# A decode kernel with attention cache and MLP: fewer loads of the output weights, another order of the last matmuls, and bias loads moved

## The chip, the cores and the metric

The kernel runs on one core of a Trainium2 chip. The metric is the device time of one execution in microseconds (us). The engines of the core run side by side: TensorE (PE) does matmuls, VectorE (DVE), ScalarE (ACT) and GpSimd (POOL) the elementwise work, and SyncE (SP) issues nearly all transfers from device memory. Those transfers run on 16 DMA engines that the core has to itself.

## The reference

One token for each of 8 sequences. `x` (8 x 448) goes through two branches whose results are mixed with a gate:

```
g = sigmoid((x * gate_w).sum(-1))
a = attention(x, k_cache, v_cache, wq, wo)   # 16 query heads, 8 key heads of 256,
                                             # the last 1024 of 4096 cache rows, softmax
b = gelu(layernorm(x) @ w1 + b1) @ w2 + b2   # 448 -> 1792 -> 448
out = g * a + (1 - g) * b                    # 8 x 448, bf16
```

All inputs are bf16. The parts of the two caches that are read are eight loads of 4096 KB each; `wq` and `wo` have 3584 KB each. In all 77.69 MB are read, and each byte of the caches is used for one sequence only.

## The kernel before

**Loads and the ring.** A ring of four large SBUF buffers (`slot`, 4 MB each) takes the loads in the order of a list (`plan`, lines 163 to 180): `wq`; eight blocks of keys (`quarter_loader`, L120), from the fifth on in turn with the values of one sequence each (`pair_loader`, L130); the remaining values; `w1`; the last values together with `w2` (`last_values`, L159); and `wo` in several pieces. `pump` (L103) issues the next load of the list on SP as soon as a buffer has been given back by `done`. SP runs its queue in order, so a load that waits holds up all behind it. A completion of a load is signalled through one of eight semaphores, which the loads take in turn; a load that takes a semaphore waits until the one that had it before has landed, unless SP knows that already.

**`wo`.** It is used as 32 chunks of 128 rows: four blocks (`q`) of 8 chunks (`J8`). `cuts` (L172) says which chunks come in one load: each of the first two blocks is one load of 896 KB, the third comes in two of 448 KB, the fourth in pieces of 2, 4, 1 and 1 chunks.

**Biases.** `biases` (L193) issues on SP `b2`, broadcast to 8 rows of `b2_b` in two loads of 4 rows, and `b1` in four loads of one row. It is called in the main loop at the second key block (L661, `m == 1`). They are first read in `norm` (L318), long after.

**Main loop** (L659). Each key block is turned on PE, or on DVE and POOL, into `kt` (`transpose_keys`), scored against all queries (`scores`), and from the fifth block on (`KQ` = 4) the softmax and the values of an earlier sequence follow (`steps`, `values`). For each sequence, `finish` and `spread` put the attention result into `oP`, in the layout in which it is a stationary operand. `mlp_hidden` (L593) makes `hs`, the 14 hidden chunks of the MLP branch, already scaled by 1 - g.

**The end** (L688 to 740). The output is a sum of 46 products: 14 chunks of `hs` by `w2` and 32 of `oP` by `wo`. `chunks` lists them in that order. All but the last `TAIL` = 12 are "wide": a matmul of 448 columns each, accumulated in four groups of PSUM partitions of `A1` in turn. When they are done, DVE adds the groups' tile and `b2s` into `accs` (L719). The last 12 are "narrow": each is two matmuls of 224 columns, one for each half of the output, into `A2[0]` or `A2[1]` as the list `part` says. Both are pieces of the one PSUM tile `S_ps`. A product `pick` by `accs` (fp32), put in at place `EARLY` of the narrow list, adds the four groups of the wide part. When the last product for `A2[1]` is done, DVE copies it to `early` (L737); at the very end DVE adds `A2[0]` and `early` into `res` (L738), and two stores write the halves (L740).

**Fillers.** `run_on(n)` (L698) issues matmuls with no use into a PSUM tile `warm`; `FILL` says after how many wide chunks how many of them come, and one of 256 columns stands ahead of the copy to `early`.

Of the kernel before, what the change touches and what calls it, by code (L numbers as in the profile page):

```python
# [12 lines left out]
F32 = mybir.dt.float32  # L13
# [4 lines left out]
def kernel(  # L18
# [15 lines left out]
    nc = tc.nc  # L34
    P = nc.NUM_PARTITIONS

    NB, Sq, D = A_x.shape
# [8 lines left out]
    QD = 4  # L46
    BL = P // QD
# [10 lines left out]
    QN = 512  # L58
# [5 lines left out]
    DO = D // 2  # L64
    J8 = Dh // BL
    NQW = Hq // QD
# [6 lines left out]
    CK = SLOT // Dh  # L73
    KQ = W // (KS * CK)
    HR = GROUP * UR
    TAIL = 12
    SHIFT = 96
    EARLY = 4
    TURNED = {5: 3, 6: 3, 7: 3}
    FAR = -3.0e38  # L80
    FILL = {0: 3, 14: 5, 22: 4, 30: 1, 34: 1}
    qscale = float(Dh) ** -0.5

    xf = A_x.rearrange("b s d -> (b s) d")
# [3 lines left out]
    consts = ctx.enter_context(tc.tile_pool(name="consts", bufs=1))  # L88
# [3 lines left out]
    work = ctx.enter_context(tc.tile_pool(name="work", bufs=1))  # L92
    spool = ctx.enter_context(tc.tile_pool(name="spool", bufs=2))
    ps_s = ctx.enter_context(tc.tile_pool(name="ps_s", bufs=1, space=PSUM))
    ps_kt = ctx.enter_context(tc.tile_pool(name="ps_kt", bufs=3, space=PSUM))
# [17 lines left out]
    def add(key, loader):  # L113
        index[key] = len(plan)
        plan.append(loader)

    def slot(*key):
        return slots[index[key]]
# [49 lines left out]
    for b in range(KQ, NB - 1):  # L168
        add(("v", b), pair_loader(A_v_cache, b))
    add(("w12",), rows_loader([w1_m, w1_t]))  # L170
    add(("v", NB - 1), last_values)
    cuts = [(q, 0, J8) for q in range(NQW - 2)] + [  # L172
        (NQW - 2, 0, 4),
        (NQW - 2, 4, 8),
        (NQW - 1, 0, 2),
        (NQW - 1, 2, 6),
        (NQW - 1, 6, 7),
        (NQW - 1, 7, 8),
    ]
# [7 lines left out]
    b2_b = consts.tile([NB, D], BF16)  # L187
# [2 lines left out]
        g_b[:], gate_w.rearrange("(o d) -> o d", o=1).to_broadcast([NB, D])  # L190
    )

    def biases():  # L193
        for o in range(0, NB, QD):
            nc.sync.dma_start(
                b2_b[o : o + QD, :],
                B_b2.rearrange("(o d) -> o d", o=1).to_broadcast([QD, D]),
            )
        parts = B_b1.rearrange("(t d) -> t d", t=QD)
        for t in range(QD):  # L200
            nc.sync.dma_start(b1_r[BL * t : BL * t + 1, :], parts[t : t + 1, :])

    ident = consts.tile([P, P], BF16)
    make_identity(nc, ident[:])
# [3 lines left out]
    S_ps = ps_s.tile([P, NG * W], F32)  # L208
# [19 lines left out]
    for u in range(NG):  # L228
        o = u * BL
# [31 lines left out]
    mask = consts.tile([P, QD, rep], F32)  # L261
    gall = consts.tile([P, NB], F32)
    oall = consts.tile([P, NB], F32)
    pick = consts.tile([P, NB], F32)
    om = consts.tile([NB, 1], F32)
    b1_b = consts.tile([P, FQ], BF16)

# [8 lines left out]
    def gate():  # L276
        prod = consts.tile([NB, D], F32)
        gl = consts.tile([NB, 1], F32)
        nc.vector.scalar_tensor_tensor(
            prod[:],  # L280
            in0=x_sb[:],
            scalar=1.0,
            in1=g_b[:],
            op0=ALU.mult,
            op1=ALU.mult,
            accum_out=gl[:],
        )
        gth = consts.tile([NB, 1], F32)
        nc.scalar.activation(gth[:], gl[:], ACT.Tanh, scale=0.5)
        nc.vector.tensor_copy(  # L290
            perm[:].rearrange("p (s a) -> p s a", a=QD),
            ident[:].rearrange("p (a s) -> p s a", a=QD),
        )
        nc.vector.reduce_sum(
            pick[:],
            ident[:].rearrange("p (g b) -> p b g", g=QD)[:, 0:NB, :],
            axis=AXIS.X,
        )
        nc.vector.reduce_sum(
            mask[:],  # L300
            ident[:]
            .rearrange("p (s o a) -> p a o s", a=QD, o=1)
            .to_broadcast([P, QD, rep, SK]),
            axis=AXIS.X,
        )
        nc.vector.tensor_scalar(
            g32[0:NB, 0:1], gth[:], 0.5, 0.5, op0=ALU.mult, op1=ALU.add
        )
        nc.vector.tensor_scalar(om[:], gth[:], -0.5, 0.5, op0=ALU.mult, op1=ALU.add)
        gt = consts.tile([BL, BL], F32)  # L310
        nc.vector.transpose(gt[:], g32[:])
        gb = consts.tile([BL, BL], F32)
        nc.vector.stream_shuffle(gb[:], gt[:], [0] * BL)
        for i in range(QD):
            nc.scalar.copy(gall[BL * i : BL * (i + 1), :], gb[:, 0:NB])
        nc.vector.tensor_scalar(oall[:], gall[:], -1.0, 1.0, op0=ALU.mult, op1=ALU.add)
# [34 lines left out]
    def turn_blocks(m):  # L351
        kn = slot("k", m)[:].bitcast(F32)
        n = TURNED.get(m, 1) * CB
        B = epool.tile([P, n, QD, BL], F32, tag="B", name="B")
        nc.vector.transpose(  # L355
            B[:].rearrange("p c w x -> p (c w x)"),
            kn[:, 0 : n * P],
        )
        blocks[m] = B
# [14 lines left out]
    def transpose_keys(m, between):  # L374
        kn = slot("k", m)[:].bitcast(F32)
        kt = ktpool.tile([P, P, CK, NJ], BF16, tag="kt", name="kt")
        KT[0] = kt
        n = TURNED.get(m, 1)
        for g in range(CK // CB):
            if g < n:  # L380
                if g == 0:
                    spread_blocks(m, kt)
                for step in between.get(g, ()):
                    step()
                continue
            ktp = ps_kt.tile([P, CB, P, NJ], BF16, tag="ktp", name="ktp")
            words = ktp[:].bitcast(F32)
            for c in range(CB):
                o = (g * CB + c) * P
                nc.tensor.transpose(words[:, c, :, 0], kn[:, o : o + P], ident_f[:])  # L390
            dst = kt[:, :, g * CB : (g + 1) * CB, :]
            src = ktp[:].rearrange("p c x t -> p x c t")
            if g in BY_ACT[m // KQ]:
                nc.scalar.copy(dst, src)  # L394
            else:
                nc.vector.tensor_copy(dst, src)  # L396
            for step in between.get(g, ()):
                step()
        done()
# [76 lines left out]
    def top(g):  # L476
        nmx = spool.tile([P, 1], F32, tag="nmx", name="nmx")
        nc.vector.reduce_max(nmx[:], S_ps[:], axis=AXIS.X, negate=True)  # L478
        soft[-1 - g] = nmx
# [161 lines left out]
    def steps(b):  # L641
        if b == 0:
            return {
                3: [lambda: expo(0, 0)],
                5: [lambda: expo(0, 1)],
                8: [lambda: turn(0)],
                10: [lambda: scale(0)],
                12: [lambda: bring(0)],
            }
        return {  # L650
            5: [lambda: scale(b)],
            7: [lambda: bring(b)],
            9: [lambda: finish(b - 1)],
            12: [lambda: spread(b - 1)],
        }
# [3 lines left out]
    for m in range(NK):  # L659
        transpose_keys(m, steps(m - KQ) if m >= KQ else {})  # L660
        if m == 1:  # L661
            biases()
        if m < KQ:
            turn_blocks(m + 1)
        if m == 0:
            gate()
        scores(m)
        if m % KQ == KQ - 1:
            top(m // KQ)
        if m >= KQ:  # L670
            values(m - KQ)
# [13 lines left out]
    finish(b)  # L685
    spread(b)

    A2 = [S_ps[:, k * QN : k * QN + DO] for k in range(2)]  # L688
    warm = ps_kt.tile([P, QN], F32, tag="ktp", name="warm")
    w2 = slot("w12")  # L690
    w = slot("wo")
# [3 lines left out]
    ] + [(oP[:, c % J8, c // J8, :], w[:, c * D : (c + 1) * D]) for c in range(NCH)]  # L695
    wide, narrow = chunks[:-TAIL], chunks[-TAIL:]

    def run_on(n, m=QN):  # L698
        for _ in range(n):
            nc.tensor.matmul(  # L700
                warm[:, 0:m],
                lhsT=ident[:],
                rhs=slot("v", NB - 1)[:, 0:m],
                start=True,
                stop=True,
            )

    run_on(FILL[0])
    for i, (lhsT, rhs) in enumerate(wide):
        g = i % QD  # L710
        nc.tensor.matmul(
            A1[BL * g : BL * g + NB, :],
            lhsT=lhsT,
# [3 lines left out]
        )  # L717
        run_on(FILL.get(i + 1, 0))
    nc.vector.tensor_tensor(accs[:], A1[:], b2s[:], op=ALU.add)  # L719
    narrow.insert(EARLY, (pick[:], accs[:]))  # L720
    part = [1, 0, 1, 0, 0, 1, 1, 0, 0, 0, 0, 0, 0]
    early = consts.tile([2 * BL, DO], F32)
    res = consts.tile([2 * BL, DO], BF16)
    for i, (lhsT, rhs) in enumerate(narrow):
        k = part[i]
        for h in range(2):
            g = 2 * k + h
            nc.tensor.matmul(
                A2[k][BL * g : BL * g + NB, :],
                lhsT=lhsT,  # L730
                rhs=rhs[:, h * DO : (h + 1) * DO],
                start=(k not in part[:i]),
                stop=(k not in part[i + 1 :]),
            )
        if 1 not in part[i + 1 :] and k == 1:
            run_on(1, QN // 2)
            nc.vector.tensor_copy(early[:], A2[1][2 * BL : P, :])  # L737
    nc.vector.tensor_tensor(res[:], A2[0][0 : 2 * BL, :], early[:], op=ALU.add)  # L738
    for h, eng in enumerate((nc.sync, nc.scalar)):
# [31 lines left out]
```

## Time and profile before

| | us |
|---|---|
| median of 3 runs | 189.43 |
| lowest and highest run | 189.4, 189.66 |
| the profiled execution, its own time | 189.29 |
| span of its instructions | 187.4 |
| PE busy (share of the span) | 125.4 (67%) |
| DVE busy | 94.0 (50%) |
| POOL busy | 80.8 (43%) |
| ACT busy | 72.4 (39%) |
| wo, loads of 896 KB, 448 KB, 224 KB, 112 KB | 2, 3, 1, 2 of them |

The span is the time from the first to the last instruction in the profile; the whole execution is 1.9 us longer. Busy shares are averages over stages with different limits. In the page's slices each digit is the busy share of one fortieth of the span in tenths, with 9 for 90% and more; "DMA" is the mean over the 16 DMA engines. In the chain of waits each step is followed back to what released it. In the timeline a line gives start, duration, engine, source line, operation, output and inputs, and in brackets how long the engine was idle before and what ended that.

### The profile page before, as it was taken

The numbers are of one execution on the slowest core, as the hardware profiler recorded it, in microseconds if no ns is written. First come the engines' busy times: TensorE is split into PE (matmuls) and PEld (weight loads), VectorE is DVE, ScalarE is ACT, GpSimd is POOL, SyncE is SP. The second block draws the span as 40 slices with busy tenths as digits, with TensorE's granted clock in tenths as the row PEclk, the third lists the DMA queues.
The fourth block names the chain that finished last, engine by engine and source line by source line (L and its number), as shares of the span: only waits on it lengthen the run. The fifth ranks groups of instructions, "written<-read, shape, count | busy, mean of one in ns | idle before, by whom it ended". The sixth has DMA issues, their size and how long they took to land.

```text
span 187.4 us, 2775 instructions
## 1 busy us (share of the span) xinstructions
PE 125.4 (67%) x1102; PEld 73.0 (39%) x1103; DVE 94.0 (50%) x161; ACT 72.4 (39%) x87; POOL 80.8 (43%) x157
## 2 busy tenths in 40 slices
PE   0252498998988988489877985984670167543983
PEld 0010485675756746253752572563120022111321
DVE  6602247664654566770662281493044982347611
ACT  2003379692855929740680373184025010001000
POOL 8401591671927639103996899299900000000000
PEclk9999579999999999756997899999576576855798
DMA  6999999999998999999999999999999999999991
GB/s 223 444 455 448 448 434 413 388 442 448 444 448 381 418 439 435 430 416 455 451 416 402 434 458 441 392 441 427 430 430 423 434 430 428 432 430 418 421 406 65
DMA packets 5443, 77.85 MB, mean 415 GB/s; under 512 B 540, under 2 KB 1080, under 8 KB 1848
## 3 DMA queue, kind: packets, MB, share of 16 engines
q1 hardware_dynamic: 5384, 77.68, 97.2%
q8 instruction: 8, 0.13, 0.2%
q10 hardware_dynamic: 48, 0.02, 0.0%
q14 instruction: 3, 0.02, 0.0%
HBM read 77.69 MB, written 0.01 MB: 415 GB/s over the span
## 4 chain that ended last, share of the span: by engine, by line
DMA 46%; PE 25%; ACT 12%; DVE 7%; POOL 5%; issue 2%; SPq 1%; POOLq 0%; ACTq 0%; DVEq 0%
DMA slot<-in_A_k_cache_dram 22%; PE ktp L390 15%; DMA slot<-in_B_w_dram 12%; DMA slot<-in_A_wo_dram 12%; ACT kt L394 9%; PE S_ps L465 7%; POOL kt L369 5%; DVE kt L396 3%; PE PO L550 2%; DVE B L355 1%; ACT E L489 1%; ACT other L489 1%; SPq L143 1%; DVE EB L505 1%; DVE E L503 1%
## 5 line engine op out<-in xcount | busy, mean ns | idle before, releaser
L369 POOL COPY kt<-B 32x128 f32<-32x128 f32 (+1 forms) x128 | 72.4, 566 | 42.8 <-PE S_ps L465 24.9
L390 PE MATMUL ktp<-ident_f,slot 128*128 128x128 f32 x456 | 64.6, 292 | 14.0 <-DMA slot<-in_A_k_cache_dram 5.9
L394 ACT COPY kt<-ktp 128x1024 bf16<-128x1024 bf16 x57 | 56.3, 1015 | 45.8 <-PE ktp L390 45.7
L390 PEld LDWEIGHTS ktp<-ident_f,slot 128*128 128x128 f32 x456 | 52.4, 148 | 27.7 <-ACT kt L394 11.3
L396 DVE COPY kt<-ktp 128x1024 bf16<-128x1024 bf16 x57 | 39.0, 689 | 32.0 <-PE ktp L390 31.6
L465 PE MATMUL S_ps<-kt,qw 128*16 128x512 bf16 x256 | 21.1, 458 | 12.1 <-POOL kt L369 9.3
L550 PE MATMUL PO<-slot,ET 128*16 128x512 bf16 x256 | 22.2, 508 | 6.6 <-DMA slot<-in_A_v_cache_dram 3.0
L355 DVE STREAM_TRANSPOSE B<-slot 128x512 f32<-128x512 f32 (+1 forms) x8 | 8.8, 1105 | 14.2 <-DMA slot<-in_A_k_cache_dram 9.7
L465 PEld LDWEIGHTS <-qw 128*16 128x16 bf16 x256 | 6.6, 92 | 23.8 <-issue 13.3
L550 PEld LDWEIGHTS <-ET 128*16 128x16 bf16 x256 | 7.9, 112 | 19.3 <-issue 12.9
L525 PE MATMUL sm<-EZ,perm 128*128 128x128 bf16 x8 | 2.0, 248 | 13.4 <-DVE EZ L512 13.4
L407 PE MATMUL S_ps<-slot,xw 128*8 128x512 bf16 x24 | 2.9, 618 | 10.7 <-DVE xw L254 7.1
L478 DVE TENSOR_REDUCE nmx<-S_ps 128x1 f32<-128x2048 f32 x2 | 4.6, 2292 | 9.8 <-PE S_ps L465 9.8
L565 DVE STREAM_TRANSPOSE T<-PO 128x512 f32<-128x512 f32 x8 | 5.7, 707 | 7.6 <-PE PO L550 7.6
L627 ACT ACTIVATE zb<-za 128x448 f32<-128x448 f32 x1 | 0.6, 576 | 18.8 <-DVE za L626 18.8
L489 ACT ACTIVATE E<-S_ps,nmx 128x1024 f32<-128x1024 f32 x2 | 4.1, 2031 | 9.7 <-DVE nmx L478 9.7
L525 PEld LDWEIGHTS <-perm 128*128 128x128 bf16 x8 | 0.8, 100 | 16.6 <-DVE EZ L512 16.6
L445 POOL COPY qw<-qt 32x64 bf16<-32x64 bf16 x8 | 2.2, 277 | 11.3 <-DVE qt L432 11.0
L533 DVE TENSOR_TENSOR ET<-sm,mask 128x512 bf16<-128x512 f32 x8 | 5.5, 687 | 1.1 <-PE sm L525 1.0
L432 DVE STREAM_TRANSPOSE qt<-qs 128x512 bf16<-128x512 bf16 x2 | 1.3, 690 | 8.8 <-ACT qs L429 8.8
L407 PEld LDWEIGHTS <-xw 128*8 128x8 bf16 x24 | 0.7, 100 | 12.0 <-POOL b_r L237 7.1
L700 PE MATMUL warm<-slot,ident 128*128 128x512 bf16 (+1 forms) x14 | 4.3, 392 | 0.1
(91 smaller groups left out, 69.0 us busy)
## 6 DMA issues: line engine op xcount, KB each, us to landing
slot<-in_A_k_cache_dram SPq DMA_DIRECT2D x8, 4096.0 KB, 24.6
slot<-in_A_v_cache_dram SPq DMA_DIRECT2D x8, 4096.0 KB, 30.0
slot<-in_A_wq_dram SPq DMA_DIRECT2D x1, 2048.0 KB
slot<-in_A_wo_dram SPq DMA_DIRECT2D x2, 896.0 KB
slot<-in_B_w_dram SPq DMA_DIRECT2D x1, 1568.0 KB
slot<-in_B_w_dram SPq DMA_DIRECT2D x1, 1344.0 KB
slot<-in_A_wo_dram SPq DMA_DIRECT2D x3, 448.0 KB, 22.1
slot<-in_A_wq_dram SPq DMA_DIRECT2D x1, 1024.0 KB
```

The lines of the kernel that those rows point to most:

```text
L355: nc.vector.transpose(B[:].rearrange("p c w x -> p (c w x)"), kn[:, 0 : n * P],)
L369: nc.gpsimd.tensor_copy(words[BL * w : BL * (w + 1), BL * g : BL * (g + 1), 0:n, 0], B[BL * g : BL * (g + 1), :, w].rearrange("p c x -> p ...
L390: nc.tensor.transpose(words[:, c, :, 0], kn[:, o : o + P], ident_f[:])
L394: nc.scalar.copy(dst, src)
L396: nc.vector.tensor_copy(dst, src)
L465: nc.tensor.matmul(S_ps[BL * t : BL * t + HR, k * QN : (k + 1) * QN], lhsT=qf[:, o : o + HR], rhs=KT[0][:, x : x + n, :, j], start=False, ...
L478: nc.vector.reduce_max(nmx[:], S_ps[:], axis=AXIS.X, negate=True)
L489: nc.scalar.activation((E[:, 0:W], other[:])[u].rearrange("p (c k s) -> p k s c", k=KQ, c=NCK), S_ps[:].rearrange("p (k u s c) -> p u k s ...
L533: nc.vector.tensor_tensor(ET[:].rearrange("p c u a r -> p (c u) a r"), sm[:] .rearrange("p k (o r) -> p k o r", o=1) .to_broadcast([P, NCK ...
L550: nc.tensor.matmul(PO[BL * t : BL * t + Hq], lhsT=ET[:, c].rearrange("p u a r -> p (u a r)"), rhs=vn[:, c], start=(c < QD), stop=(c >= NCK ...
L565: nc.vector.transpose(T[:, 0 : NG * n], PO[:].rearrange("p u (e j) -> p u j e", j=J8))
L700: nc.tensor.matmul(warm[:, 0:m], lhsT=ident[:], rhs=slot("v", NB - 1)[:, 0:m], start=True, stop=True,)
```

## The change

The third block of `wo` comes in one load and the first six chunks of the fourth in one. Sixteen chunks are narrow instead of twelve, so the wide part ends with the second block of `wo`; the product with `accs` comes first among the narrow ones, and with `pick` widened to 32 columns (the further 24 zero) it writes all 32 partitions of its groups. The third block's chunks go to `A2[0]` and `A2[1]` in turn, the fourth's first chunk to `A2[1]`, the rest to `A2[0]`. `A2[1]` is a PSUM tile of its own (`other`). The fillers 30:1 and 34:1 become 30:4, and the half filler comes after the third block. `b1` stays at the second key block; `b2` comes in four loads of two rows, issued at the fifth key block. `early` takes a work buffer, and a tile `rest` that is not used keeps the addresses of what follows.

```diff
-    TAIL = 12
+    TAIL = 16
     SHIFT = 96
-    EARLY = 4
+    EARLY = 0
...
-    FILL = {0: 3, 14: 5, 22: 4, 30: 1, 34: 1}
+    FILL = {0: 3, 14: 5, 22: 4, 30: 4}
...
-    cuts = [(q, 0, J8) for q in range(NQW - 2)] + [
-        (NQW - 2, 0, 4),
-        (NQW - 2, 4, 8),
-        (NQW - 1, 0, 2),
-        (NQW - 1, 2, 6),
+    cuts = [(q, 0, J8) for q in range(NQW - 1)] + [
+        (NQW - 1, 0, 6),
         (NQW - 1, 6, 7),
         (NQW - 1, 7, 8),
     ]
...
-    def biases():
-        for o in range(0, NB, QD):
-            nc.sync.dma_start(
-                b2_b[o : o + QD, :],
-                B_b2.rearrange("(o d) -> o d", o=1).to_broadcast([QD, D]),
-            )
+    def bias1():
         parts = B_b1.rearrange("(t d) -> t d", t=QD)
         for t in range(QD):
             nc.sync.dma_start(b1_r[BL * t : BL * t + 1, :], parts[t : t + 1, :])
+
+    def bias2():
+        for o in range(0, NB, 2):
+            nc.sync.dma_start(
+                b2_b[o : o + 2, :],
+                B_b2.rearrange("(o d) -> o d", o=1).to_broadcast([2, D]),
+            )
...
-    pick = consts.tile([P, NB], F32)
+    pick = consts.tile([P, BL], F32)
+    nc.gpsimd.memset(pick[:], 0.0)
...
-            pick[:],
+            pick[:, 0:NB],
...
         if m == 1:
-            biases()
+            bias1()
+        if m == KQ:
+            bias2()
...
-    A2 = [S_ps[:, k * QN : k * QN + DO] for k in range(2)]
+    other = ps_kt.tile([P, QN], F32, tag="ktp", name="other")
+    A2 = [S_ps[:, 0:DO], other[:, 0:DO]]
...
-    part = [1, 0, 1, 0, 0, 1, 1, 0, 0, 0, 0, 0, 0]
-    early = consts.tile([2 * BL, DO], F32)
+    part = [1] + [0, 1] * 4 + [1] + [0] * 7
+    early = work.tile([2 * BL, DO], F32, tag="w1", name="early")
+    consts.tile([P, DO - BL + NB], F32, name="rest")
...
-                A2[k][BL * g : BL * g + NB, :],
+                A2[k][BL * g : BL * g + lhsT.shape[-1], :],
...
+        if i == J8:
+            run_on(1, QN // 2)
         if 1 not in part[i + 1 :] and k == 1:
-            run_on(1, QN // 2)
             nc.vector.tensor_copy(early[:], A2[1][2 * BL : P, :])
```

## The prediction

> **What bounds the kernel now.** I read the page's slices and queues first, then the chain that ended last, then the last five microseconds instruction by instruction, then SP's waits.
>
> ```profile
> span 187.4 us, 2775 instructions
> ...
> PEclk9999579999999999756997899999576576855798
> DMA  6999999999998999999999999999999999999991
> GB/s 223 444 455 448 448 434 413 388 442 448 444 448 381 418 439 435 430 416 455 451 416 402 434 458 441 392 441 427 430 430 423 434 430 428 432 430 418 421 406 65
> ...
> q1 hardware_dynamic: 5384, 77.68, 97.2%
> q8 instruction: 8, 0.13, 0.2%
> ```
>
> The DMA row never leaves 9 (one 8) until the last slice: the 77.68 MB of loads set the pace. The last pieces of the chain of waits, in order of time (start, duration, what):
>
> ```profile
> 139.89 22.30 DMA slot<-in_B_w_dram
> 162.19 0.02 issue
> 162.21 21.60 DMA slot<-in_A_wo_dram
> 183.81 0.04 issue
> 183.85 0.84 PE S_ps L728 x12
> 184.69 0.02 issue
> 184.71 0.38 DVE res L738
> ```
>
> So the end is: wo lands, twelve narrow matmuls, one DVE addition, the store. The timeline there:
>
> ```profile
> 181.46 0.62 DVE L719 TENSOR_TENSOR accs<-S_ps,b2s 128x448 f32<-128x448 f32 x1 [3.18 <-PE S_ps L711]
> ...
> 183.15 0.39 DVE L737 COPY early<-S_ps 64x224 f32<-64x224 f32 x1 [1.06 <-PE S_ps L728]
> ...
> 183.85 0.82 PE L728 MATMUL S_ps<-slot,oP 128*8 128x224 bf16 x12 [0.52 <-DMA slot<-in_A_wo_dram]
> 184.71 0.38 DVE L738 TENSOR_TENSOR res<-S_ps,early 64x224 bf16<-64x224 f32 x1 [1.17 <-PE S_ps L728]
> ```
>
> From the trace's landing signals (one from each of the 16 DMA engines per load; us from the span's start) I take, for the wo loads in order, when the first and the last engine reported:
>
> ```
> load, KB            first   last
> block 1, 896        176.12  177.80
> block 2, 896        178.27  179.94
> block 3a, 448       179.36  181.01
> block 3b, 448       180.46  182.11
> block 4, 224        181.03  182.71
> block 4, 448        182.13  183.81
> block 4, 112        182.45  184.09
> block 4, 112        182.74  184.37
> ```
>
> Successive loads follow with no gap, and the last engine is steadily 1.6 to 1.7 us behind the first. Adding the packet durations of an engine from the start (64 packets of 32768 B at 1213 ns, some 136 of 16384 B at 611 ns, the smaller ones; each overlaps the next by about 3.5 ns) brings the first engine to about 182.4, where its last signal is at 182.74: it never idles. The late ones are explained by the q8 line: each of the 8 instruction fetches (16384 B, 881 to 962 ns) puts a pause of 863 ns before one engine's next data packet and stretches it by some 550 ns (1764 against 1213), 1.41 us in all, and each falls on another engine.
>
> **The change part by part.**
>
> *Block 3 in one load, six groups of block 4 in one.* 128 packets of 3584 B twice become 128 of 7168 B; 1792 and 3584 B become 5376 B. The records have 74, 140 and 272 ns for 1792, 3584 and 7168 B; 5376 B lies in the middle, 206 ns. An engine carries 8 rows: 8 x (2 x 140 - 272) = 0.064 us, and 8 x (74 + 140 - 206) = 0.064 us, 0.13 us. By landings it is less: 1.07 + 1.10 for the halves against 2.14 for a whole block is 0.03, and 0.57 + 1.10 (first engine) against the 1.62 that 8 x (206 - 3.5) gives is 0.05; 0.08 us. I take 0.09, bounds 0.08 and 0.13. The last landing comes at 184.28 and that of the six groups at 183.72.
>
> *The tail on TensorE.* After its last wait on a large wo piece the old kernel has 4 groups, so 4 pairs of matmuls, then one pair for each small load. Pairs start at 183.850, 183.946, 184.042, 184.137, 184.233: 0.096 us apart; the last pair starts at 184.410, 0.04 after its landing, not after its predecessor. In the new kernel all six groups wait for one landing: six pairs start from 183.72 + 0.04 = 183.76, the seventh and eighth have landed by then (184.00, 184.28), so the last pair starts at 183.76 + 7 x 0.096 = 184.43. Bounded by landing alone it would start at 184.32. So TensorE becomes the bound of the last 0.6 us and takes the 0.09 back: +0.02 in place of -0.09. Both ends kept.
>
> *Second accumulator, `early`.* Its last pair is now the first pair after the six-group landing: matmul end 183.77 + 0.26, the copy from 184.07 to 184.46 (0.39, L737's row), beside TensorE writing the other tile; `res` starts 0.30 after the last pair (184.712 - 184.413), at 184.73. Hidden with 0.27 us to spare; uncovered it would cost at most the 0.39.
>
> *Twelve to sixteen narrow chunks, `pick` first, fillers 4 in place of 1 and 1.* The wide part ends with block 2's eight chunks at 180.57; `accs` follows, 180.61 to 181.24 (0.62). Four fillers take 1.04 (the four at 179.05), to 181.54. The `pick` matmuls then need 0.40 (from 182.355 to the next pair at 182.753): 181.94, before block 3 lands at 182.07. The load of 32 stationary columns for 8 lies between the rows of 0.09 for 8 columns and 0.10 for 128. Block 3's eight pairs run from 182.11 to 182.88, the half filler (0.28) to 183.16. All of this is over 0.56 us before the six groups land; that wait hides it. The queue order is kept, so what stands behind `pick`'s wait on `accs` is block 3's matmuls, which wait longer anyway.
>
> *b1, b2 and SP's queue.* SP's largest waits of concern here (waited for: us in total, times, longest):
>
> ```profile
> SPq L143 <- DMA slot<-in_A_v_cache_dram: 9.8, 2, 9.4
> SPq L126 <- DMA slot<-in_A_k_cache_dram: 9.4, 1, 9.4
> ...
> SPq L201 <- DMA slot<-in_A_k_cache_dram: 6.4, 1, 6.4
> ...
> SPq L143 <- DMA slot<-in_B_w_dram: 4.8, 3, 3.4
> ```
>
> Every load takes the next of eight completion semaphores and waits for the load that had it eight before. Two b2 issues (0.83 at 43.55) go; the 6.4 us wait in b1 and the 9.4 us of the sixth key load go with them, since the counting moves by two; so do the waits of the last two wo loads (9.4, 3.4), which now stand behind w1 (161.6, 162.2) and are issued by about 162.5 instead of 171.97 and 175.69. The sixth key load is issued about 55 to 58 rather than 61.46, the second value load about 66 rather than 71.15, both bounded by their slots. None of this moves an engine: in each case the loads ahead had not finished, and the DMA row is full there. The four b2 issues come behind the seventh key load (82.64 to 83.2) and ahead of the third value load, which waits until 89.16; four at 0.26 to 0.53 are at most 2.1 us, so it hides them. Their semaphores were last held by loads that landed by 71.1. b2 is first read at 152.1.
>
> *Small loads on few engines.* In the trace a b2 load of four rows is signalled by 4 engines and a b1 load by 1, the same one. Between the value load's signals at 69.4 and the key load's at 79.1 the engine that carried all six lost 0.55 us against the untouched ones, those with two lost 0.1 to 0.25. It ends 0.90 us behind the first engine; the ones that b2 touches end at about 0.6 to 1.31, none among the eight at 1.44 to 1.65. If two-row loads run on two engines, one of them carries eight small packets and one four. At 0.55/6 = 0.09 each that is +0.18 on the worst, 1.08: nothing. At the 0.18 us between b1's landings (70.31, 70.49, 70.67, 70.86) it is 0.35 + 8 x 0.18 = 1.79, so 0.12 over today's last. I take 0 (the loss as measured is nearer), bound +0.12.
>
> The Trainium skill ("DMA: Bandwidth & Descriptors", section "Why a DMA increments its semaphore by 16 and not by 1") says that such a load runs on the lowest-numbered k of the 16 engines, k set by the outer dimension. That speaks against this part: by it the two-row loads would sit on the very engine of b1. The trace agrees for k = 4 and 1 (b1's engine is one of b2's four); k = 2 no run here shows yet. By that rule the sum stays the same, by the price above.
>
> *The memset of `pick`* on POOL follows one that ends at 6.96 and costs between 0 and the 0.50 us of that one, which writes fourteen times the elements. The first matmul at 7.14 may wait for it; the query's last weights land at 11.67, which hides it.
>
> **Sum.** -0.09 (loads) + 0.11 (the tail that TensorE now sets) + 0 = +0.02 us, between -0.13 and +0.14. The profiled execution took 189.29 us (187.4 of span, 1.9 around it), 0.14 below the median of the three shown, 189.43. 189.31 on the one scale, 189.45 on the other; I say 189.4. Within 0.2% (0.38 us) is about what a measurement of this kernel can tell from no change.
>
> **The rivals.**
>
> *A fetch on an engine that is already late (slower).* The last load lands with its slowest engine. Today no fetch falls on an engine that carried b2 or b1. If, with the small loads spread otherwise or twelve more matmul and weight instructions on PE, one falls on the engine with eight small packets, it ends at 1.08 + 1.41 = 2.49 behind the first, 0.8 after today's last: 190.2. It decides once an engine is over 1.67 late. For it: 8 of 16 engines are hit, blindly as far as I see. Against: up to 172 us the order on PE is unchanged, and the hits on eight different engines look like a rotation.
>
> *The tail at half clock (slower).* The sixteen matmuls now bind; at half clock a pair takes 0.19, and 7 x 0.096 = 0.67 more goes to the end: 190.1. It decides if the granted clock falls before 184.5. For it: the PEclk row has 5s wherever PE waits. Against: the clock is 1.00 from 176.1 to 186.3 now, changing in steps of 3.41 us after stretches in which PE was busy less than half, and the new fillers leave PE idle only 183.2 to 183.8.
>
> *A better balance (faster).* The sixteen lags average 1.06 us, the last is 1.65. If the moved small loads and the freer SP let the late engines catch up, 0.59 + 0.09 is to be had, less 0.02 that stays on TensorE: 188.7 to 188.8. For it: the spread is the only slack in the load stream. Against: the late engines are those of the fetches, which the change does not touch, and loads give each engine fixed rows.
>
> *The landing bound holds to the end*: -0.09, 189.3; too small to be told apart, so part of the forecast's case.
>
> **How the numbers follow.** Forecast 0.5 (its own range 189.1 to 189.7), the fetch 0.22, the half clock 0.08, the balance 0.2. Faster by over 0.2%: 0.2; within: 0.5; slower: 0.3. The range takes in the fetch's and the clock's case and the nearer part of the balance: 188.8 to 190.2.
>
> **What would show it.** Block 3 in one step of 2.14 on each engine; the six groups' landing near 183.7, the last pair 0.67 us after the first with the last landing before it; `early` between them, ahead of `res`; SP without the 9.4 us waits at L126 and the wo loads; the last engine 1.6 to 1.7 behind the first. Wrong would be: a lag over 2 us on an engine of b2, a last pair that still waits for its landing, a clock below 1.00 after 180 us, or a gap between loads.

## The result, and the profile after

The changed kernel is slower by a quarter of a per cent. Its median is 189.75 us over 22 runs (189.54 to 191.19), against 189.45 for the kernel before over 22 runs (189.31 to 189.87); the ratio over all runs is 1.0025, with a 95% interval of 1.0013 to 1.0037. The quotient of the two medians is only 1.0016: five of the 22 runs are slower than the others by a good deal, and count in the ratio. The forecast was 189.4 and no change that can be told; the interval excludes no change at all, though its lower end lies within the 0.2% that the prediction counted as none.

The page of the changed kernel, in the lines that answer to those of before:

```profile
span 187.8 us, 2791 instructions
...
PEclk9999579999999999756997899999576555785798
DMA  6999998999998999999999999999999999999991
...
q1 hardware_dynamic: 5096, 77.68, 97.0%
q8 instruction: 8, 0.13, 0.2%
```

The same 77.68 MB in 288 fewer packets, a DMA row that is as full, and the same eight instruction fetches on q8. The last pieces of the chain of waits (start, duration, what):

```profile
160.86 23.28 DMA slot<-in_A_wo_dram
184.14 0.04 issue
184.18 0.26 PE other L732 x2
184.44 0.67 PE S_ps L732 x14
185.14 0.38 DVE res L743
```

The end has the shape of before: `wo` lands, narrow matmuls, one addition. The timeline there (start, duration, engine, line, operation; in brackets the idle time before and what ended it):

```profile
181.06 0.62 DVE L722 TENSOR_TENSOR accs<-S_ps,b2s 128x448 f32<-128x448 f32 x1 [2.24 <-PE S_ps L714]
...
184.18 0.26 PE L732 MATMUL other<-slot,oP 128*8 128x224 bf16 x2 [0.84 <-DMA slot<-in_A_wo_dram]
...
184.18 0.91 PE L732 MATMUL S_ps<-slot,oP 128*8 128x224 bf16 x14
184.48 0.39 DVE L742 COPY early<-other 64x224 f32<-64x224 f32 x1 [2.80 <-PE other L732]
185.14 0.38 DVE L743 TENSOR_TENSOR res<-S_ps,early 64x224 bf16<-64x224 f32 x1 [0.26 <-PE S_ps L732]
```

Everything here stands 0.4 us later than before, but not because of the loads. This one execution is already 0.4 late at 50 us: the first signal of the third key load comes at 40.61 instead of 40.26, and packets of 32768 B between 20 and 30 us took 1238 ns on average instead of 1213. Over the 22 runs the spans, which are on record to 0.1 us, go from 187.3 to 188.0 with a median of 187.5; in other comparisons below the kernel before has 187.4 to 188.1 with a median of 187.6. So the span did not grow.

What grew is what lies around the span. The profiled execution took 191.19 us: 3.4 more than its span, where the kernel before had 1.9. The page is silent on it, since it ends with the span. The view of the DMA queues in the window from 187.5 to 193 us shows it (queue, packets, MB, share of 16 engines). The kernel before:

```profile
DMA packets 0, 0.00 MB, mean 0 GB/s; under 512 B 0, under 2 KB 0, under 8 KB 0
```

The changed kernel:

```profile
DMA packets 2, 0.02 MB, mean 4 GB/s; under 512 B 0, under 2 KB 0, under 8 KB 0
...
q8 instruction: 1, 0.02, 1.6%
q14 instruction: 1, 0.01, 0.5%
```

Two instruction fetches after the kernel's work is done: 8192 B at 189.46 for 436 ns, 16384 B at 190.01 for 1414 ns. In 17 of the 22 runs the time beyond the span is 2.14 to 2.35 us, in the other 5 it is 2.88 to 3.39.

The trace does not say for which engine a fetch is. Two engines' programs had grown by more than one instruction: DVE's as built from 185 to 188 (the traces have one record more, 186 and 189), since `norm` (L332, L333) now waits for four `b2` loads instead of two; PE's from 1769 to 1781, by six more loads of weights and six more matmuls. POOL's grew by one, the memset of `pick`.

### The profile page after: what moved, and what is told of

Its sections match the earlier page's. It is cut to its first block, busy times and chain, and to the rows that moved or that the text cites. A ratio compares the mean times of both kernels' runs of the same rounds, so it can differ in the third digit from the quotient of the medians.

```text
span 187.8 us, 2791 instructions
## 1 busy us (share of the span) xinstructions
PE 125.6 (67%) x1109; PEld 73.3 (39%) x1109; DVE 94.5 (50%) x161; ACT 72.3 (39%) x87; POOL 81.1 (43%) x158
## 3 DMA queue, kind: packets, MB, share of 16 engines
q1 hardware_dynamic: 5096, 77.68, 97.0%
## 4 chain that ended last, share of the span: by engine, by line
DMA 35%; PE 28%; ACT 14%; DVE 12%; POOL 5%; issue 2%; SPq 1%; POOLq 0%; ACTq 0%; DVEq 0%
DMA slot<-in_A_k_cache_dram 22%; PE ktp L390 15%; DMA slot<-in_A_wo_dram 12%; ACT kt L394 9%; PE S_ps L465 7%; POOL kt L369 5%; PE PO L550 5%; DVE kt L396 3%; ACT E L489 2%; ACT other L489 2%; DVE EB L505 1%; DVE B L355 1%; SPq L143 1%; DVE nmx L478 1%; DVE E L503 1%
## 5 line engine op out<-in xcount | busy, mean ns | idle before, releaser
L550 PE MATMUL PO<-slot,ET 128*16 128x512 bf16 x256 | 23.2, 526 | 6.4 <-DMA slot<-in_A_v_cache_dram 2.8
```

The costliest lines, as they stand in the source:

```text
L550: nc.tensor.matmul(PO[BL * t : BL * t + Hq], lhsT=ET[:, c].rearrange("p u a r -> p (u a r)"), rhs=vn[:, c], start=(c < QD), stop=(c >= NCK ...
```

## The experiments

**Theories.** By the main one the loss is the two fetches. It has two parts: PE's twelve instructions bring one (theory P), DVE's three the other (theory D). The rivals: the moved loads make the last landing later (theory L), or each added instruction costs some time at the end, wherever a fetch falls (theory N). Each kernel computes the whole output. The column "beyond the span" has the time of each run less its own span, which is on record to 0.1 us, so that a scatter of 0.1 within a row means nothing; the kernel before, in the 130 runs beside these, has 1.86 to 1.96, median 1.9.

| run | DVE, PE instructions | median us (n) | ratio to before, 95% interval | median span | beyond the span |
|---|---|---|---|---|---|
| after | 188, 1781 | 189.75 (22) | 1.0025 (1.0013 to 1.0037) | 187.5 | 2.14 to 2.35; 5 runs 2.88 to 3.39 |
| e1 | 185, 1781 | 189.6 (11) | 1.0008 (0.9999 to 1.0017) | 187.7 | 1.89 to 1.97; 3 runs 2.09 to 2.45 |
| e2 | 188, 1769 | 189.75 (11) | 1.0013 (1.0004 to 1.0022) | 187.6 | 2.14 to 2.24 |
| e3 | 188, 1769 | 189.95 (11) | 1.002 (1.0011 to 1.0029) | 187.8 | 2.14 to 2.21 |
| e4 | 188, 1769 | 189.84 (11) | 1.0017 (1.0007 to 1.0026) | 187.7 | 2.13 to 2.23 |
| e5 | 185, 1769 | 189.54 (11) | 1.0002 (0.9994 to 1.0011) | 187.6 | 1.87 to 1.95 |
| e6 | 185, 1781 | 189.6 (12) | 1.0011 (1.0001 to 1.0022) | 187.6 | 1.87 to 1.98; 3 runs 2.07 to 2.84 |
| e7 | 185, 1769 | 189.66 (11) | 1.0008 (0.9999 to 1.0016) | 187.7 | 1.87 to 1.96 |
| e8 | 185, 1769 | 189.74 (12) | 1.0018 (1.0009 to 1.0027) | 187.85 | 1.84 to 1.93 |
| e9 | 184, 1781 | 189.41 (11) | 1.0005 (0.999 to 1.0019) | 187.5 | 1.77 to 1.92; 4 runs 2.36 to 2.98 |
| e10 | 205, 1769 | 189.72 (12) | 1.0011 (1.0001 to 1.002) | 187.95 | 1.77 to 1.85 |
| e11 | 208, 1781 | 189.57 (12) | 1.0008 (0.9993 to 1.0024) | 187.65 | 1.76 to 1.95; 3 runs 2.11 to 2.75 |
| e12 | 185, 1829 | 189.65 (12) | 1.0009 (1.0 to 1.0018) | 187.65 | 1.88 to 1.93; 3 runs 2.41 to 2.49 |
| e13 | 184, 1841 | 189.41 (11) | 0.9994 (0.9986 to 1.0003) | 187.5 | 1.78 to 1.93 |
| e14 | 188, 1841 | 189.75 (11) | 1.0018 (1.0009 to 1.0027) | 187.6 | 2.14 to 2.31 |
| e15 | 184, 1769 | 189.51 (11) | 0.9998 (0.999 to 1.0007) | 187.7 | 1.76 to 1.86 |

### First four: which part brings the loss

e1 is the kernel before with six more weight loads and matmuls on PE that add nothing to the output (in `bring`, for the last sequence):

```diff
-        nc.tensor.matmul(
+        for _ in range(7 if b == NB - 1 else 1):
+            nc.tensor.matmul(
```

> The kernel before with the matmul that brings the last sequence's probabilities (L525) issued seven times instead of once: six more weight loads and six more matmuls on PE, the same number that the change adds, while PE waits for the last values. The loads are untouched. Theory P (the time is lost after the span: PE's program, twelve instructions longer, crosses the border of a block, and a fetch of 16384 B follows at the end, as at 190.01 us in the changed kernel's profile and nowhere in the old one's): time less span goes from 1.9 us to 2.2 or more, the ratio to the kernel before is about 1.0015 to 1.003, span 187.4 as before, and the profile has a packet of 16384 B on the instruction queue after the span. Theory D (it is the three more instructions on DVE, and the fetch of 8192 B at 189.46): 1.000, 1.9 us outside. Theory L (the moved bias loads make the load stream longer): 1.000.

e2 is the kernel before with three more instructions on DVE:

```diff
-    nc.vector.memset(eps_t[:], 1e-5)
+    for _ in range(4):
+        nc.vector.memset(eps_t[:], 1e-5)
```

> The kernel before with the small memset of eps_t (L221) issued four times instead of once: three more instructions on DVE, as many as the change adds there (its extra semaphore waits), at the start, where DVE waits for the first loads anyway. Theory D: time less span 2.2 us or more instead of 1.9, ratio 1.0015 to 1.003, and a packet of 8192 B on the instruction queue after the span. Theory P: 1.000, 1.9 us outside, no such packet. Theory L: 1.000.

e3 is the kernel before with the change's `bias1` and `bias2` and their two calls, and nothing else of it:

```diff
...
-            biases()
+            bias1()
+        if m == KQ:
+            bias2()
```

> The kernel before with the bias part of the change alone: b2 in four loads of two rows at the fifth key block, b1 alone at the second. DVE has the three more waits, PE's program is as before. Theory L: the last wo landing is later than 184.4 by 0.3 us or more, span 187.7 or more, ratio about 1.002. Theory D: span 187.4, time less span 2.2, ratio 1.0015 to 1.003. Theory P: span 187.4, 1.9 outside, ratio 1.000.

e4 is the changed kernel with twelve instructions of fillers less on PE:

```diff
-    FILL = {0: 3, 14: 5, 22: 4, 30: 4}
+    FILL = {0: 3, 14: 4, 22: 3, 30: 1}
...
-        if i == J8:
-            run_on(1, QN // 2)
```

> The changed kernel with six filler matmuls fewer (14:4, 22:3, 30:1, and no half filler): twelve PE instructions fewer, so PE's program is as long as in the kernel before; loads and DVE are as in the changed kernel. Theory P: time less span falls from 2.2 to 1.9, the time to 0.1 us under the kernel before (the wo loads end 0.1 sooner), ratio 0.9990 to 1.000. Theory D and theory L: as the changed kernel, ratio about 1.0025, with 2.2 us outside (D) or a span of 187.7 or more (L).

Three repeated memsets on DVE, all of them done long before, make the kernel before as slow in the median as the changed one. e2 after its span:

```profile
DMA packets 1, 0.01 MB, mean 1 GB/s; under 512 B 0, under 2 KB 0, under 8 KB 0
...
q14 instruction: 1, 0.01, 0.6%
```

One packet of 8192 B, at 189.25, without the change's memset on POOL. The ratio, 1.0013, lies a little under the 1.0015 expected. e3 and e4 have the same packet (at 189.35 and 189.17), and all 33 runs of the three lie at 2.13 to 2.24 beyond the span. e1 has a 16384 B fetch at 188.76 instead, and in only 3 of 11 runs was the time beyond the span above 2. So the small fetch goes with DVE's three instructions, and its price is there in every run; the large one goes with PE's twelve and costs only some runs. (In e1's profile the last matmuls also come late: `res` starts 0.52 us after the last landing, where 0.34 is usual. That is in its span, not beyond it.) Theory L does not hold: e3, with the moved loads, has its last landing at 184.52, and a copy of the kernel before (e5) at 184.68.

e3 is slower than e2, and that is another matter. At the end SP waits for the eight completion semaphores in a fixed order, and the last wait is on the stores (waited for: us in total, times, longest). In the kernel before, then in e3:

```profile
SPq L766 <- DMA out_dram<-res: 0.7, 1, 0.7
```

```profile
SPq L770 <- DMA out_dram<-res: 1.0, 1, 1.0
```

The waits go by pairs of semaphores. In the kernel before the first three pairs are done at 185.49, 185.56 and 185.62, and the stores have the last two (186.39 and 186.57): the others are asked for while the stores fly. In e8, below, the stores have the first two pairs (186.54 and 186.74), and the other three follow them at 186.80, 186.87 and 186.93. e3 issues two more loads than the kernel before, which moves the stores in the same way: from the last store's landing to the end it is 0.83 us before and 1.01 in e3. The changed kernel issues 4 + 4 + 6 loads for `b1`, `b2` and the pieces of `wo`, where the kernel before had 4 + 2 + 8: the same 14, so its stores stay where they were.

### Second four: the parts by themselves

e5 is the kernel before unchanged. e6 is the changed kernel with `biases` of before at `m == 1`. e7 is e6 with the fillers of e4. e8 is e4 with `b2` in one load:

```diff
-        for o in range(0, NB, 2):
+        for o in range(0, NB, NB):
             nc.sync.dma_start(
-                b2_b[o : o + 2, :],
-                B_b2.rearrange("(o d) -> o d", o=1).to_broadcast([2, D]),
+                b2_b[o : o + NB, :],
+                B_b2.rearrange("(o d) -> o d", o=1).to_broadcast([NB, D]),
             )
```

> The kernel before, unchanged: how far two sets of runs of one program lie apart, and a second profile of it. All theories: ratio 1.000 with an interval of about 0.001 on each side, span 187.4 to 187.6, time less span 1.9, no packet on an instruction queue after the span. If the span is 187.5 or 187.6 here, the first profile's 187.4 was at the lower end and the spans of the changed kernel's runs (median 187.5) are no longer than before.

> The changed kernel with the biases loaded as before: wo in six loads and the new order of the last matmuls (twelve more PE instructions), DVE's program as long as in the kernel before. Theory P: a fetch of 16384 B after the span, 2.2 us outside; the wo loads give 0.1 us back, ratio 1.000 to 1.002. Theory D (only DVE's longer program costs time): 1.9 outside, ratio 0.9990 to 0.9998. Theory L (the bias loads lengthen the stream): the same as D.

> As the last, with six filler matmuls fewer (14:4, 22:3, 30:1, no half filler): neither PE's nor DVE's program is longer than before. Theories P and D together: no fetch after the span, 1.9 us outside, and the 0.1 us of the wo loads stays: ratio 0.9990 to 0.9998, 189.3 to 189.45 us, under both kernels. Theory F (the fillers are needed to hold the clock, or the late copy to early delays the end): ratio 1.000 or more though 1.9 is outside, with the last pair of matmuls more than 0.05 us after the last landing.

> The changed kernel with six fillers fewer and b2 at the fifth key block in one load of eight rows: PE's and DVE's programs as long as in the kernel before, b2 still late. Theories P and D: as the last, 1.9 us outside, ratio 0.9990 to 0.9998. Theory L (the place of b2's loads costs time): slower than the last by 0.1% or more with a later last landing.

With DVE back at 185 instructions, about 1.9 beyond the span is back in e7 and e8 in all 23 runs, and in 9 of 12 of e6, whose PE still has 1781. That is what theory D and theory P say. The profiled execution of e6 is one of those 9, and in it no fetch follows the span: PE's late fetch itself comes in some executions only. But none of the three became faster than before, as had been hoped, for two reasons that had not been thought of. All three issue another number of loads, and from the last store's landing to the end e6, e7 and e8 took 0.97, 0.96 and 1.03 instead of 0.83. SP's last wait in e8:

```profile
SPq L769 <- DMA out_dram<-res: 1.1, 2, 0.9
```

And the fillers left out can be missed. In the profiled execution of e7, by windows (stretch, then PE, its weight loads, DVE, ACT and POOL busy, granted clock, DMA share, GB/s) and in the timeline:

```profile
180.97:184.38 3.41, 1.75 (x33) 0.89 (x34) 0.68 (x2) 0.00 (x0) 0.00 (x0) 1.00 0.73 287
```

```profile
183.99 1.15 PE L728 MATMUL S_ps<-slot,oP 128*8 128x224 bf16 x14
...
185.18 0.38 DVE L737 TENSOR_TENSOR res<-S_ps,early 64x224 bf16<-64x224 f32 x1 [0.50 <-PE S_ps L728]
```

PE was busy 1.75 of these 3.41 us, and at 184.38 the granted clock fell to 0.5: the last matmul took 391 ns instead of 260, and `res` starts 0.68 after the last landing (184.50) where 0.35 is usual (185.14 after 184.79 in the changed kernel), 0.3 us lost. In e4 and e8 the same fillers are left out, and there the granted clock stays at 1.00 past the end of the matmuls and `res` starts 0.35 after the last landing; e4's stretch, with PE busy 1.88 us:

```profile
181.10:184.50 3.40, 1.88 (x35) 1.06 (x35) 0.80 (x2) 0.00 (x0) 0.00 (x0) 1.00 0.64 251
```

So this loss is shown for one execution of e7; how many of its runs have it is not known.

### Third four: away from the border, and over it

If DVE's fetch is a border in its program, then one instruction less than before must be as good, and many more must be good as well, since the fetch then falls inside the span. By theory N many more would be worse. e9 is the changed kernel with work taken off DVE; e10 and e11 put twenty memsets after `norm` into the kernel before and into the changed one; e12 puts 30 matmuls without use after `query` into the kernel before:

```diff
-    nc.vector.memset(eps_t[:], 1e-5)
+    nc.gpsimd.memset(eps_t[:], 1e-5)
...
-        turned(0, nc.vector.tensor_copy, nc.vector.tensor_copy)
+        turned(0, nc.scalar.copy, nc.vector.tensor_copy)
```

```diff
             norm()
+            for _ in range(20):
+                nc.vector.memset(eps_t[:], 1e-5)
```

```diff
     query()
+    extra = ps_kt.tile([P, QN], F32, tag="ktp", name="extra")
+    for _ in range(30):
+        nc.tensor.matmul(
+            extra[:, 0:P], lhsT=ident[:], rhs=ident[:], start=True, stop=True
+        )
```

> The changed kernel with four DVE instructions fewer: the memset of eps_t goes to POOL, the first copies of x (L242, L246) to ACT, all at the start, where the weights of the query are still loading. Loads, matmuls and fillers are as in the changed kernel; DVE's program is one shorter than in the kernel before. Theory D (the three added DVE instructions bring a fetch after the span): 1.9 us outside in the profile, no packet of 8192 B after the span, 189.35 to 189.55 us, ratio 0.9990 to 1.0005. Theory P (PE's twelve): as the changed kernel, ratio 1.0015 to 1.0025.

> The kernel before with the memset of eps_t issued twenty times more on DVE, after norm at about 152 us, where DVE waits for values. Theory D, as a border: with twenty more instructions the block border is crossed well before DVE's last instructions, so the fetch of 8192 B falls inside the span (at 165 to 184 us) and nothing waits for it at the end: 1.9 us outside, ratio 1.000 to 1.001, less than with three more (1.0013). Theory N (each DVE instruction has its price at the end, where semaphores or records are cleared): 2.2 us outside or more, ratio 1.0013 or more.

> The changed kernel, complete, with the same twenty memsets on DVE after norm. Theory D, as a border: the fetch moves into the span, 1.9 us outside, 0.2 us or more faster than the changed kernel though it does more work: 189.4 to 189.6, ratio 0.9992 to 1.0006. Theory N or theory P: ratio 1.002 or more, 2.2 us outside.

> The kernel before with thirty idle matmuls of 128 columns on PE after the query, at about 13 to 16 us, where PE waits for the first keys: sixty more PE instructions. Theory P, as a border: the ninth fetch of 16384 B comes inside the span, before 184 us, nothing waits for it after the span, 1.9 us outside; on an engine that is already late it would cost up to 1.4 us, on one of the clean ones nothing: ratio 1.000 or 1.005 and more. If PE's length plays no part at the end: ratio 1.000, 1.9 outside. Theory N for PE (a price for each instruction): ratio over 1.001 with 1.9 us inside and 2.2 outside.

Theory N falls: with 205 and 208 instructions on DVE the time beyond the span is 1.77 to 1.85 and mostly 1.76 to 1.95, lower than before. The fetch is there, but in the span: e10 in the window from 171 to 175 us, on q14 at 172.73 (the one on q8 is the eighth large fetch, at 171.11):

```profile
q8 instruction: 1, 0.02, 1.5%
q14 instruction: 1, 0.01, 0.5%
```

(in e11 it is at 173.43). Only DVE's program differs from that of the kernel it was made from, so the small fetch is DVE's. It starts when DVE has begun 188 of its 206 records in the trace of e10 and 191 of 209 in e11; the changed kernel has 189 in all, the kernel before 186. In e10's profile it fell on a DMA engine that was late already: the last engine is 1.70 us behind the first for the load that lands from 170.37 on, 2.25 for the next and 2.11 for the last, whose landing ends at 185.00, and the median span is 187.95. So e10, against e2, lost in the span what it gained at the end. Its ratio, 1.0011, and e11's, 1.0008, lie just over what was expected. In e9 the small fetch is gone; the large one is left, at 188.68, in 4 of 11 runs:

```profile
q8 instruction: 1, 0.02, 1.6%
```

Seven runs of e9 lie at 189.29 to 189.47, those four at 189.86 to 190.48; the profiled execution is one of the four. e11's, with as many PE instructions, is not one of its three slow runs and has no such fetch. In e12 the ninth 16384 B fetch stands at 184.22, inside the span, yet 3 of 12 runs still took 2.41 to 2.49 beyond theirs.

### Last three: the changed kernel without either fetch

e13 is e9 with the 30 matmuls of e12, e14 the changed kernel with them, e15 is e9 with twelve PE instructions of early fillers less (`FILL = {0: 1, 14: 1, 22: 4, 30: 4}`), so that PE has 1769 as before.

> The changed kernel with DVE's program shortened as in e9 and the thirty idle matmuls of e12 on PE after the query: neither engine's program crosses its border in its last instructions. If the slow third of e9's runs (189.86 to 190.48) is PE's fetch after the span: no packet on an instruction queue after the span, 1.9 us outside, all but one or two runs between 189.25 and 189.7, median 189.3 to 189.45, ratio 0.9985 to 0.9998. If it is something else: a third of the runs over 189.8 as in e9, ratio 1.000 or more.

> The changed kernel, complete, with the thirty idle matmuls on PE after the query; DVE keeps its three more instructions. If PE's fetch makes the changed kernel's runs with 2.9 us and more outside (5 of 22): the packet of 8192 B is there after the span, that of 16384 B is not, 2.2 us outside, no run over 190.3, median 189.65 to 189.8, ratio 1.001 to 1.0018. If not: runs of 190.4 and more as before.

> The changed kernel with DVE's program shortened as in e9 and six of the early fillers left out (0:1, 14:1; the last eight and the half one stay): PE's and DVE's programs no longer than in the kernel before. If the borders are all that costs: 1.9 us outside, median 189.3 to 189.45, ratio 0.9985 to 0.9998, a version faster than both kernels. If the early fillers are needed for the clock: a granted clock of 0.5 somewhere after 178 us in the profile, the last pair more than 0.1 us after the last landing, ratio 1.0003 or more.

e13 and e14 were timed side by side and differ in DVE's 184 against 188 instructions alone (with the work that went to other engines): 189.41 and 189.75, with 1.82 and 2.16 in the median beyond the span. So the 0.34 between the medians all lies beyond the span; some 0.27 of it is the step from 188 to 185 that the change made (2.18 and 1.9 in the median), the rest that from 185 to 184. Both have the ninth 16384 B fetch in the span (e13's at 183.98), and no run of either is over 190.01, where the changed kernel had 7 of 22. e15 removes both fetches the other way and has none of 11 runs above 1.86.

e13 has the whole change and neither fetch: 0.9994, interval 0.9986 to 1.0003. Its mean is 0.12 us under that of the kernel before beside it, and 0.09 of this lies beyond the span (1.83 against 1.91 in the mean), which comes with DVE's 184 instructions; the spans differ by 0.04 in the mean. So the 0.1 that the loads save can't be told apart in the time of a run. No version here beats the kernel before by more than its interval. e15 was expected at 189.3 to 189.45 and took 189.51, with a median span of 187.7. Its profiled execution, whose span is that median, has one DMA engine 2.06 us behind the first at the last load, where e13's has 1.78: the lag is 1.92 for the load that lands from 137.26 on and 2.18 for the next, with a 16384 B fetch at 139.43 between. So there a fetch fell on an engine that was late already; whether that is so in e15's other runs no trace shows.

## Why the prediction was wrong

**The sum is the step that failed.** It put "187.4 of span, 1.9 around it" and carried the 1.9 over unchanged. The rest was worked out to hundredths inside the span, where the change indeed did nothing harmful; the term that was taken for a constant went from 1.9 to 2.2 in 17 of 22 runs, which is DVE's fetch, and to 2.9 to 3.4 in the other 5. The profiled execution is one of the 5 and has PE's fetch as well; e14, with PE's fetch moved into the span, has no run like them. In the mean the term is 2.41, so it grew by 0.5, no less than the whole loss of 0.48 in the mean. Of the twelve PE instructions the prediction thought only as a fetch that might hit a late engine in the span; of DVE's three waits it did not think at all, though the part on `b2` counted the four loads that cause them.

The Trainium skill ("Runtime: NRT & Kernel Launch", section "Instruction fetch mechanics") says that an engine's instructions come in blocks, fetched while the ones before run, at a cost that is mostly hidden. The runs bear it out for a fetch in the span, with DVE's in e11: 189.57, no slower than the changed kernel. They do not where the fetch falls on a DMA engine that is late already (e10, above), nor for a fetch behind an engine's last work: with e2's three instructions every run has 2.14 us or more beyond the span, 0.25 us or so more than before.

**The loads** were right. By the first engine's signals the third block took 178.70 to 180.84 and the six chunks 180.84 to 182.44, together 3.74 us against 3.86 for the same 14 chunks before (178.27 to 182.13): 0.12 saved, within the bounds of 0.08 and 0.13. The last engine is 1.69 to 1.76 behind, so there was no better balance either.

**The tail on TensorE** was mis-sized: +0.11 that did not come. It counted the pairs one after the other, 0.096 us apart. But the first pair for `other` and the first for `S_ps` run side by side (starts at 184.178, 184.181, 184.184 and 184.188). They write different groups of PSUM partitions, as the pairs for the two accumulators did before, within one tile. The timeline of the kernel before had it, eight matmuls in 0.36 us, started in two groups of four at 182.157 to 182.167 and 182.252 to 182.262:

```profile
182.16 0.36 PE L728 MATMUL S_ps<-slot,oP 128*8 128x224 bf16 x8 [0.42 <-DMA slot<-in_A_wo_dram]
```

So the last pair's turn would come at 184.76 (0.096 after the one before it), its chunk lands at 184.79, and it starts at 184.835. The end is still set by the landing, and TensorE takes nothing back of what the loads saved. It was the case called "the landing bound holds to the end", and the prediction had named its sign among those of being wrong: a last pair that still waits for its landing. By itself this made the sum 0.11 too high, so it worked against the term that was left out.

**The second accumulator** was right: the copy at 184.48 to 184.87 ends 0.26 before `res`, beside the matmuls. **The narrow chunks, `pick` first**: `accs` is ready at 181.68, the `pick` matmuls stand at 181.91, ahead of the third block's landing at 182.53, and PE idles again before the six chunks; hidden, as predicted.

**SP's queue** was right. Its waits after:

```profile
SPq L126 <- PE ktp L390: 41.1, 4, 15.7
...
SPq L143 <- DMA slot<-in_B_w_dram: 1.0, 2, 0.8
...
SPq L143 <- DMA slot<-in_A_v_cache_dram: 0.4, 1, 0.4
```

The 9.4 us wait at L126 for an earlier key load is gone, and those of the `wo` loads (9.8 and 4.8 in all) are 0.4 and 1.0. The sixth key load went out at 54.02, somewhat before the 55 to 58 that was forecast. No engine gained by it, as argued.

**Small loads on few engines** were right at 0. A two-row `b2` load is signalled by two engines (99.26 and 99.80 for the first) and a one-row `b1` load by one. So the trace agrees, in the case of k = 2 that the prediction had left open, with the rule of the Trainium skill cited there, in the number of engines. The engine of `b1` ends about 0.95 behind the first and sets nothing.

**The rivals.** The fetch on a late engine did not happen in the changed kernel, but e10 shows that it can: an engine 2.11 behind. The half clock did not happen either; e7, with fillers left out, shows that it can. It fell there after 1.75 of 3.41 us busy, just over the "less than half" of the prediction, and did not in e4 after 1.88 of 3.40. The better balance did not come, as said under the loads.

## What to carry to other kernels

Subtract the span from the time before explaining a small loss, and look at the window behind the span: the page does not show it. A change that adds a few instructions to an engine, semaphore waits included, can move an instruction fetch behind its last work, here at some 0.3 us for DVE's and up to 1.2 for PE's. On DVE a handful of instructions less, or twenty more placed earlier, undid it; on PE the 1769 of before did, 1829 in only 9 of 12 runs, and 1841 in all 22. And when the number of loads changes, look at which completion semaphores the final stores get.

## What the runs showed of the hardware

- **A border in DVE's program.** With 188 instructions an 8192 B fetch follows the span in every profile, and the time beyond it is 2.13 to 2.35 us but for PE's late fetches; with 185 it is 1.84 to 1.98; with 184, 205 or 208 it is 1.76 to 1.95. So the kernel before may itself lose some 0.1 us there, though no fetch is recorded behind its span; why was not settled. By the fetches of e10 and e11 the border lies at about 188 of DVE's records in the trace.
- **A border in PE's program.** With 1769 instructions no profile has a late 16384 B fetch, and no run the time for one. With 1781 three of five profiles have it (the changed kernel, e1, e9), with 3.38, 2.16 and 2.39 us beyond the span; e6 and e11 do not, with 1.89 and 1.91. By the times, 18 of the 68 runs take 0.2 to 1.2 us more; with 1829 instructions 3 of 12 do, with 1841 none of 22. Why the fetch comes in some executions only was not settled.
- **The stores' semaphores.** 0.13 to 0.2 us at the end in the profiles of e3, e6, e7 and e8, whose stores stand on other semaphores (0.96 to 1.03 from the last store's landing to the end); 0.83 to 0.85 in all the others, whose stores stand on the last two.
- **An engine's fetch in the span** puts its DMA engine back, and that sets the end when the engine is late already (e10: the last engine is 1.70 us behind the first for the load before the fetch, 2.25 for the next).
